# Stage 2's weight quarters over five chunks of stage 1, and the next chunk's tokens ahead of a chunk's last pairs

## The chip, the cores and the metric

The kernel runs on one core of a Trainium2 chip. The metric is the time of one execution on the device in microseconds, the median of several runs. The core has five engines, each with its own instruction queue that it works through in order: TensorE (PE in the profile), VectorE (DVE), ScalarE (ACT), GpSimd (POOL) and SyncE (SP), which here only issues DMAs. An engine waits on semaphores for results of the others; a waiting instruction holds up all that stands behind it in its queue.

## The reference

A windowed attention is followed by two gated feed-forward layers on its 2304 tokens. All inputs are float32.

```python
x = attention(q, k, v)                  # 4 batches, 8 heads, 576 positions, head size 64 -> [2304, 512]
a = x @ w1; b = x @ w2                  # 512 -> 1024
y = (a * b @ w3) @ w_out                # 1024 -> 1024 -> 512          (stage 1)
g = y @ w_gate; v2 = y @ w_val          # 512 -> 1536
out = (g * sigmoid(g) * v2) @ w_out2    # 1536 -> 512                  (stage 2)
```

## The kernel before

Every float32 matrix is split into a high and a low float32r part, and each product is made of three matmuls (high by high, high by low, low by high: `mm3`, L207 to L212). The high part is an ACT copy and the low part a subtraction, on DVE for tokens (`to_parts`, L156) and on POOL for weights.

The attention runs in units of a head pair: scores (PE), softmax (DVE, ACT, POOL), transposes (PE, with an ACT copy `pt` behind each), values (PE). Four head pairs are one batch of 576 tokens. The output of a head pair is written to the DRAM tensor `x1d` (L390); the first batch goes into `x` directly.

Stage 1 takes the tokens in five chunks, 0 to 4, of 512, 512, 512, 512 and 256 (`stage1`, eight steps `k` each). A step makes a gate on PE into one bank (`gate_a`, copied out by ACT as `ta`), a second into another (`gate_b`, multiplied by DVE, split into `p`), and 12 matmuls of the contraction of the step before. The contracted weights `W` were made of `w3` and `w_out` earlier. Results go to the DRAM tensor `x2d`. Between the gates of chunks 0 to 2 stand the attention units of batches 1 to 3, so that a batch is done at three quarters of a chunk. A chunk's tokens `x` are loaded from `x1d` into a raw buffer (`raw<-x1d`, L148) once that batch is written (`x1_there`), and split by `next_block` (ACT copies and DVE subtractions of 128x1024, two of each).

Stage 2 multiplies 2 x 2 blocks by seven products in place of eight (Strassen's scheme in Winograd's form). The seven sums of each weight block have to be made first: `quarters` takes one pair of weight blocks (`wg`, `wv` or `wo2`) from a raw buffer, rebuilds its float32 values from 64-bit input (ACT L193, DVE L194 and L195), adds quarters (DVE, L524 to L527), splits the results into a stage buffer (ACT L507, POOL L508) and stores them in DRAM (`wd` or `wod`, L545). There are 18 pairs, three for each of six blocks. In stage 2 a ring of 14 buffers is filled from `wd` (`fill`, L643), and `operands` makes the seven token operands from `x2d`, which needs both raw buffers.

Two things set the order around the change. The list `blocks` says in which order pairs and tokens are loaded; only two raw buffers exist after chunk 0 (three up to there), and a load is issued when a raw buffer comes free (`done_with`, `load_block`). And `rest(k)` and `replace(k)`, called behind each step of a chunk, take pieces of work from the queue `work`, three or two a step, the rest of a chunk's work in its last step. On DVE each piece stands behind the step's `p` (`tc.issue_after`). Within these bounds a scheduler at build time sets the order on each engine.

Of the kernel before, what the change touches and what calls it, by code (L numbers as in the profile page):

```python
# [11 lines left out]
F32R = mybir.dt.float32r  # L12
# [11 lines left out]
P = 128  # L24
# [8 lines left out]
K1 = F1 // P  # L33
# [19 lines left out]
N_W1 = len(W_ORDER)  # L53
for _k in range(0, K2, 2):
    W_ORDER += [(("wg", _k), ("wg", _k + 1)), (("wv", _k), ("wv", _k + 1)), (("wo2", _k), ("wo2", _k + 1))]
NW = len(W_ORDER)
# [25 lines left out]
NRING = 14  # L82

UNITS = [1, 1, 1, 1, 1, 1, 2]

def moe_chain_kernel(tc, q_in, k_in, v_in, w_in, mask_in, out):
# [8 lines left out]
    with static as st, other as ot, psum as pp, dram as dp:  # L97
# [18 lines left out]
        count = {"att": 0, "p": 0, "o": 0}  # L116


        blocks = [("w", i) for i in range(N_W1)] + [("x1", 1)]
        for c in (1, 2, 3):  # L120
            blocks += [("w", i) for i in range(N_W1 + 6 * (c - 1), N_W1 + 6 * c)] + [("x1", c + 1)]
        blocks += [("x2", (c, j)) for c in range(NC2) for j in range(2)]
        n_loaded, n_split = [0], [0]
        slot_of, pair_of, uses, raw_at = {}, {}, {}, {}
# [140 lines left out]
        with att1_pool as a1, att2_pool as a2:  # L265
# [6 lines left out]
            raw_pool = tc.tile_pool(name="rawx", bufs=1)  # L272
# [184 lines left out]
            for s in range(2 * K1):  # L457
                h, j = divmod(s, K1)
# [6 lines left out]
                for kk in range(4):  # L465
                    c = slice(kk * P, (kk + 1) * P)
# [13 lines left out]
            def stage1(c, between, after):  # L480
                first, n = CHUNKS[c]
                x = xb[c % 2][:, :, :, :n]
                for k in range(K1):
                    gate_a(("w1", k), x, n, AF.Copy)
                    between(3 * k + 1)
                    p = gate_b(("w2", k), x, n)
                    between(3 * k + 2)
                    flush()
                    between(3 * k + 3)

                    def fin(k=k, p=p):
                        contract(slot_of["W", k], p, n, k == 0, k == K1 - 1)
                        if k == K1 - 1:
                            drain(lambda m: x2d[m, :, first:first + n], n)

                    pend.append(fin)
                    after(k)

            def attend_in(c):
                lo, hi = done_at[c + 1], done_at[c + 2]  # L500
                return lambda n: attend(lo + math.ceil((hi - lo) * n / (3 * K1 * ATT_BY)) if n < 3 * K1 * ATT_BY else hi)
# [55 lines left out]
                    except StopIteration:  # L557
                        work.popleft()

            def rest(k):  # L560
                while n_split[0] < N_W1 and free:
                    next_block()
                for b in range(1, B):
                    if at[0] >= done_at[b + 1]:
                        x1_there.update({b} if b < B - 1 else {b, b + 1})
                load_block()
                if n_split[0] > N_W1:
                    if k == 0:
                        work.extend([quarters() for _ in range(6)])
                    step(99 if k == K1 - 1 else 3)  # L570
                if k == K1 - 1:
                    next_block()

            for c in range(3):
                stage1(c, attend_in(c), rest)
                if c == 0:
                    raw_pool.__exit__(None, None, None)
                    stage_pool = tc.tile_pool(name="stages", bufs=1)
                    sp = stage_pool.__enter__()
                    stages.extend(sp.tile([P, 1792], F32R, name=f"stage{i}") for i in range(2))  # L580
            stage_pool.__exit__(None, None, None)


# [2 lines left out]
        with mid_pool as mp:  # L586
# [57 lines left out]
                    n_ring[0] += 1  # L644

            def replace(k):
                if k == 2:
                    work.append(operands())
                if k >= 2:
                    step(99 if k == K1 - 1 else 2)  # L650

                fill({5: 10, 6: 12, 7: NRING}.get(k, 9))

            stage1(3, lambda n: None, rest)
            stage1(4, lambda n: None, replace)
            flush_first = pend.pop()
            fill()
# [184 lines left out]
```

## Time and profile before

| | us |
|---|---|
| median of 3 runs (lowest, highest) | 893.24 (892.51, 894.55) |
| the profiled execution | 895.88 |
| its span, first to last instruction | 894.1 |
| PE busy in it | 859.2 (96%) |
| DVE, ACT, POOL busy | 567.2, 351.4, 166.8 |
| chunk 0 of stage 1 on PE | about 98 to 187 |
| chunk 1, chunk 2 | 187 to 276, 276 to 362 |
| chunk 3, chunk 4 | 362 to 435, 435 to 481 |
| stage 2 | to the end |

The attention's scores start near 9 us, and up to 98 us `W` is made. An instruction's row names its line, its engine, its operation and what it writes and reads; in brackets stands how long the engine sat idle before it and what ended that. The granted clock is a share of TensorE's full 2.4 GHz.

### The profile page before, as it was taken

Reading aid. Unit: us, or ns where it says so; the run is one execution under the profiler, and the core shown is the slowest. Engines: PE = TensorE matmul, PEld = TensorE weight load, DVE = VectorE, ACT = ScalarE, POOL = GpSimd, SP = SyncE. Lnnn points to the kernel's source line nnn. Section 1 sums busy time; section 2 is a strip of 40 time slices with the busy share of each in tenths; the row PEclk is TensorE's granted clock in tenths of the full one; section 3 lists DMA queues with packets and bytes.
Section 4 is the critical chain, followed back from the end, with each engine's and each line's share of the span. In section 5 each row is a group of like instructions: output and inputs, shape, how many; then the busy total and the mean of one; then the engine's idle time right before and its main releaser. Section 6 shows DMA issues by size and latency. Waiting matters only on the chain.

```text
span 894.1 us, 13459 instructions
## 1 busy us (share of the span) xinstructions
PE 859.2 (96%) x5065; PEld 780.3 (87%) x5066; DVE 567.2 (63%) x968; ACT 351.4 (39%) x809; POOL 166.8 (19%) x149
## 2 busy tenths in 40 slices
PE   8889899999998989899899999999999999999998
PEld 5767688878887878688799999999999999999998
DVE  5887953355555643454365866678666687666766
ACT  5866753355646553434342322232222232222221
POOL 4556531015432533143200000000000000000000
PEclk9999799999999999899999999999999999999999
DMA  9886732259787767886948766687766667766311
GB/s 296 263 278 223 231 108 63 83 181 290 249 239 266 240 214 231 299 283 224 312 160 306 243 199 206 210 283 232 243 208 212 210 200 237 247 213 204 126 48 71
DMA packets 92433, 192.95 MB, mean 216 GB/s; under 512 B 6480, under 2 KB 56272, under 8 KB 87632
## 3 DMA queue, kind: packets, MB, share of 16 engines
q1 hardware_dynamic: 89488, 187.37, 64.4%
q10 hardware_dynamic: 2880, 4.72, 1.4%
q8 instruction: 40, 0.66, 0.3%
q14 instruction: 25, 0.20, 0.1%
HBM read 150.65 MB, written 41.42 MB: 215 GB/s over the span
## 4 chain that ended last, share of the span: by engine, by line
PE 64%; DMA 17%; ACT 5%; DVE 5%; POOL 4%; issue 3%; SPq 1%; ACTq 0%; POOLq 0%; DVEq 0%
PE bk L210 20%; PE bk L211 20%; PE bk L212 20%; DMA raw<-w_in 8%; DMA raw<-x1d 3%; POOL stage L508 3%; DVE raw L195 2%; PE bk L312 2%; DMA wd<-mid 2%; DMA wd<-stage 1%; ACT raw L193 1%; DMA x1d<-o 1%; ACT s L331 1%; DVE raw L194 1%; PE bk L364 1%
## 5 line engine op out<-in xcount | busy, mean ns | idle before, releaser
L695 DVE TENSOR_TENSOR s<-bk,s 128x384 f32<-128x384 f32 x252 | 137.5, 554 | 48.9 <-PE bk L212 28.5
L210 PE MATMUL bk<-x,w 128*128 128x512 f32 (+2 forms) x368 | 139.7, 382 | 11.5 <-ACT x L157 11.3
L211 PE MATMUL bk<-x,w 128*128 128x512 f32 (+2 forms) x368 | 139.4, 379 | 1.7 <-DVE x L158 1.6
L212 PE MATMUL bk<-x,w 128*128 128x512 f32 (+2 forms) x368 | 138.3, 376 | 0.0
L212 PE MATMUL bk<-p,wo 128*128 128x384 f32 x288 | 97.3, 338 | 0.0
L210 PE MATMUL bk<-p,wo 128*128 128x384 f32 x288 | 96.8, 337 | 0.0
L211 PE MATMUL bk<-p,wo 128*128 128x384 f32 x288 | 96.8, 336 | 0.0
L737 DVE TENSOR_TENSOR acc<-bk,acc 128x384 f32<-128x384 f32 x120 | 66.5, 554 | 43.9 <-PE bk L212 43.5
L210 PEld LDWEIGHTS bk<-x,w 128*128 128x128 f32 x368 | 71.6, 196 | 23.7 <-ACT x L157 12.8
L698 ACT ACTIVATE s<-s 128x384 f32<-128x384 f32 x72 | 37.8, 526 | 129.6 <-DVE s L695 128.5
L211 PEld LDWEIGHTS bk<-x,w 128*128 128x128 f32 x368 | 71.5, 194 | 13.1 <-DVE x L158 3.5
L212 PEld LDWEIGHTS bk<-x,w 128*128 128x128 f32 x368 | 71.7, 195 | 9.9
L157 ACT ACTIVATE p<-s 128x384 fp32r<-128x384 f32 x72 | 37.7, 526 | 102.6 <-DVE s L699 102.6
L235 DVE TENSOR_TENSOR ta<-bk,ta 128x512 f32<-128x512 f32 (+1 forms) x40 | 25.4, 636 | 75.2 <-PE bk L212 47.6
L210 PE MATMUL bk<-w 128*128 128x384 f32 (+1 forms) x196 | 70.3, 366 | 2.3 <-ACT w L188 2.0
L211 PE MATMUL bk<-w 128*128 128x384 f32 (+1 forms) x196 | 69.7, 360 | 0.5 <-POOL w L189 0.5
L211 PE MATMUL bk<-w,mid 128*128 128x384 f32 x204 | 68.6, 336 | 0.0
L212 PE MATMUL bk<-w,mid 128*128 128x384 f32 x204 | 67.9, 337 | 0.0
L210 PE MATMUL bk<-w,mid 128*128 128x384 f32 x204 | 67.8, 336 | 0.0
L212 PE MATMUL bk<-w 128*128 128x384 f32 (+1 forms) x196 | 67.4, 356 | 0.0
L508 POOL TENSOR_TENSOR stage<-raw,stage 128x512 fp32r<-128x512 f32 (+2 forms) x56 | 52.4, 962 | 75.2 <-ACT stage L507 75.2
L195 DVE SCALAR_TENSOR_TENSOR raw<-raw 128x1024 uint32<-128x1024 uint32 (+1 forms) x39 | 59.2, 1519 | 9.5 <-ACT raw L193 8.2
(99 smaller groups left out, 1756.3 us busy)
## 6 DMA issues: line engine op xcount, KB each, us to landing
raw<-w_in SPq DMA_DIRECT2D x37, 1024.0 KB, 7.6
mid<-wd SPq DMA_DIRECT2D x72, 512.0 KB, 4.3
w<-wd SPq DMA_DIRECT2D x45, 512.0 KB, 3.5
wo<-wod SPq DMA_DIRECT2D x36, 512.0 KB, 4.5
wd<-stage SPq DMA_DIRECT2D x16, 896.0 KB, 6.6
wd<-mid SPq DMA_DIRECT2D x8, 896.0 KB, 5.9
v<-v_in SPq DMA_DIRECT2D x16, 432.0 KB, 5.3
q<-q_in SPq DMA_DIRECT2D x32, 160.0 KB, 6.2
```

The costliest lines, as they stand in the source:

```text
L157: nc.scalar.activation(hi, src, AF.Copy)
L193: nc.scalar.activation(hi.bitcast(F32), hi.bitcast(F32), AF.Prelu, scale=REBIAS, alpha=SIGN_UP)
L195: nc.vector.scalar_tensor_tensor(out=lo, in0=hi, scalar=3, in1=lo, op0=ALU.logical_shift_left, op1=ALU.bitwise_or)
L210: nc.tensor.matmul(ps, wh, xh, start=start, stop=False)
L211: nc.tensor.matmul(ps, wh, xl, start=False, stop=False)
L212: nc.tensor.matmul(ps, wl, xh, start=False, stop=stop)
L235: nc.vector.tensor_tensor(out=u, in0=bb[:, :n], in1=ta[:, :n], op=ALU.mult)
L312: nc.tensor.matmul(ps[:, (n - b0) * KW:(n - b0 + 1) * KW], q[:, QB + 2 * QB * n:QB + 2 * QB * (n + 1)], kk[:, n * QB:n * QB + KW], start=T ...
L508: nc.gpsimd.tensor_tensor(out=dst[:, :, 1], in0=src, in1=dst[:, :, 0].bitcast(F32), op=ALU.subtract)
L695: nc.vector.tensor_tensor(out=dst[m], in0=x[m], in1=y[m], op=ALU.add)
L698: nc.scalar.activation(u[0], u[0], AF.Silu)
L737: nc.vector.tensor_tensor(out=a, in0=ps, in1=a, op=ALU.add)
```

## The change

The 18 pairs are dealt out by the list `QUARTERS`: 3, 4, 4, 5 and 2 to chunks 0 to 4, in place of 6 each to chunks 1 to 3. In `blocks` a chunk's pairs come ahead of the next chunk's tokens, but in chunk 3 the tokens of chunk 4 come first, so that they are loaded right behind chunk 3's own and split in step 1 of chunk 3. Quarters begin in step 2 of chunk 0 (by then the stage 1 weights are converted and the third raw buffer is given up for the two stage buffers), in step 0 of chunks 1, 2 and 4 and in step 1 of chunk 3. In chunk 4 `operands` stands behind the last two pairs, and the ring is filled with 4 buffers up to step 2 and 9 from step 3, since stage buffers in `mid` overlap it.

```diff
@@ -83,6 +83,7 @@
 
 UNITS = [1, 1, 1, 1, 1, 1, 2]
 
+QUARTERS = [3, 4, 4, 5, 2]
 
 
 def moe_chain_kernel(tc, q_in, k_in, v_in, w_in, mask_in, out):
@@ -116,9 +117,15 @@
         count = {"att": 0, "p": 0, "o": 0}
 
 
-        blocks = [("w", i) for i in range(N_W1)] + [("x1", 1)]
-        for c in (1, 2, 3):
-            blocks += [("w", i) for i in range(N_W1 + 6 * (c - 1), N_W1 + 6 * c)] + [("x1", c + 1)]
+        blocks = [("w", i) for i in range(N_W1)]
+        i = N_W1
+        for c, n in enumerate(QUARTERS):
+
+            x1 = [("x1", c + 1)] if c < 4 else []
+            w = [("w", i + j) for j in range(n)]
+            blocks += x1 + w if c == 3 else w + x1
+            i += n
+        assert i == NW
         blocks += [("x2", (c, j)) for c in range(NC2) for j in range(2)]
         n_loaded, n_split = [0], [0]
         slot_of, pair_of, uses, raw_at = {}, {}, {}, {}
@@ -557,27 +564,31 @@
                     except StopIteration:
                         work.popleft()
 
-            def rest(k):
+            def rest(c, k):
                 while n_split[0] < N_W1 and free:
                     next_block()
                 for b in range(1, B):
                     if at[0] >= done_at[b + 1]:
                         x1_there.update({b} if b < B - 1 else {b, b + 1})
                 load_block()
-                if n_split[0] > N_W1:
-                    if k == 0:
-                        work.extend([quarters() for _ in range(6)])
+                begin = (2, 0, 0, 1)[c]
+                if k == begin:
+                    if c == 0:
+                        assert n_split[0] == N_W1
+                        raw_pool.__exit__(None, None, None)
+                        sp = stage_pool.__enter__()
+                        stages.extend(sp.tile([P, 1792], F32R, name=f"stage{i}") for i in range(2))
+                    if c == 3:
+                        next_block()
+                    work.extend([quarters() for _ in range(QUARTERS[c])])
+                if k >= begin:
                     step(99 if k == K1 - 1 else 3)
-                if k == K1 - 1:
+                if k == K1 - 1 and c < 3:
                     next_block()
 
+            stage_pool = tc.tile_pool(name="stages", bufs=1)
             for c in range(3):
-                stage1(c, attend_in(c), rest)
-                if c == 0:
-                    raw_pool.__exit__(None, None, None)
-                    stage_pool = tc.tile_pool(name="stages", bufs=1)
-                    sp = stage_pool.__enter__()
-                    stages.extend(sp.tile([P, 1792], F32R, name=f"stage{i}") for i in range(2))
+                stage1(c, attend_in(c), lambda k: rest(c, k))
             stage_pool.__exit__(None, None, None)
 
 
@@ -644,14 +655,13 @@
                     n_ring[0] += 1
 
             def replace(k):
-                if k == 2:
-                    work.append(operands())
-                if k >= 2:
-                    step(99 if k == K1 - 1 else 2)
-
-                fill({5: 10, 6: 12, 7: NRING}.get(k, 9))
-
-            stage1(3, lambda n: None, rest)
+                if k == 0:
+                    work.extend([quarters() for _ in range(QUARTERS[4])] + [operands()])
+                step(99 if k == K1 - 1 else 4 if k < 2 else 2)
+
+                fill({5: 10, 6: 12, 7: NRING}.get(k, 9 if k > 2 else 4))
+
+            stage1(3, lambda n: None, lambda k: rest(3, k))
             stage1(4, lambda n: None, replace)
             flush_first = pend.pop()
             fill()
```

On each engine the built program changes as follows; lines of the changed kernel are seven to ten higher. PE at the passage from chunk 1 to chunk 2, before (L312 and L349 are attention scores and transposes; `p,W` is the contraction, `x_76` the tokens of chunk 2):

```order
L212 MATMUL bk_84<-p,W_75 128x512
L210 MATMUL bk_85<-p,W_75 128x512
L211 MATMUL bk_85<-p,W_75 128x512
L212 MATMUL bk_85<-p,W_75 128x512
L349 MATMUL bk_89<-ident,s_110 96x128 x3
L210 MATMUL bk_86<-x_76,w 128x512
L210 MATMUL bk_87<-x_76,w 128x512
L349 MATMUL bk_88<-ident,s_110 96x128 x3
L211 MATMUL bk_86<-x_76,w 128x512
L212 MATMUL bk_86<-x_76,w 128x512
```

And in the changed kernel:

```order
L219 MATMUL bk_85<-p,W_75 128x512
L319 MATMUL bk_89<-k_103,q_101 128x96 x4
L217 MATMUL bk_86<-x_76,w 128x512
L319 MATMUL bk_89<-k_103,q_101 128x96
L319 MATMUL bk_88<-k_103,q_101 128x96 x3
L218 MATMUL bk_86<-x_76,w 128x512
L219 MATMUL bk_86<-x_76,w 128x512
L217 MATMUL bk_86<-x_76,w 128x512
L218 MATMUL bk_86<-x_76,w 128x512
L219 MATMUL bk_86<-x_76,w 128x512
L217 MATMUL bk_86<-x_76,w 128x512
L319 MATMUL bk_88<-k_103,q_101 128x96
```

Before, both contractions, all scores and three transposes of 96x128 stand ahead of the first matmul on `x`; now the second contraction of 12 matmuls, five of the nine score matmuls' rows and the transposes stand behind it.

SP at the same place, before (`x1d<-o_80` is the last attention output that chunk 2 needs, `raw_79<-x1d` the load of its tokens):

```order
L545 DMA wd<-stage_1386 896x1x256
L297 DMA v<-v_in 96x9x128
L545 DMA wd<-stage_1387 896x1x256
L390 DMA x1d<-o_80 128x576
L545 DMA wod<-stage_1386 128x1024
L148 DMA raw_79<-x1d 128x4x512
L545 DMA wod<-stage_1387 128x1024
```

And in the changed kernel:

```order
L552 DMA wd<-stage_1046 896x1x256
L552 DMA wd<-stage_1047 896x1x256
L155 DMA raw_79<-w_in 128x2048
L296 DMA q_100<-q_in 64x5x128 x2
L299 DMA k_102<-k_in 128x576
L304 DMA v<-v_in 96x9x128
L397 DMA x1d<-o_80 128x576
L155 DMA raw_78<-x1d 128x4x512
```

The stores of quarters have moved ahead of the outputs of the last head pair, and the token load follows its output directly.

SP at the passage from chunk 2 to chunk 3, before (from the last attention output on; `mid<-wd` are the first fills of the ring):

```order
L390 DMA x1d<-o_80 128x576
L545 DMA wd<-stage_1386 896x1x256
L545 DMA wd<-stage_1387 896x1x256
L148 DMA raw_78<-x1d 128x4x512
L545 DMA wod<-stage_1386 128x1024
L545 DMA wod<-stage_1387 128x1024
L148 DMA raw_79<-w_in 128x2048
L643 DMA mid<-wd 128x1024 x2
L148 DMA raw_78<-w_in 128x2048
L643 DMA mid<-wd 128x1024 x2
```

And in the changed kernel:

```order
L397 DMA x1d<-o_81 128x576
L552 DMA wd<-stage_1046 896x1x256
L552 DMA wd<-stage_1047 896x1x256
L654 DMA mid<-wd 128x1024 x2
L397 DMA x1d<-o_80 128x576
L654 DMA mid<-wd 128x1024 x2
L155 DMA raw_79<-x1d 128x4x512
L155 DMA raw_78<-x1d 128x4x256
L155 DMA raw_79<-w_in 128x2048
L155 DMA raw_78<-w_in 128x2048
```

The load of chunk 3's tokens is no longer behind two stores, but two of the four fills are ahead of the last attention output and two behind it, and chunk 4's tokens (128x4x256) follow chunk 3's at once.

ACT in chunk 4, before, from step 0's `ta` on (`x_67`, `w` 128x768 are stage 2's operands, from `raw` or from sums `tx`):

```order
L229 ACTIVATE ta<-bk_86 128x256
L252 ACTIVATE o_81<-bk_82 128x512
L157 ACTIVATE p<-ta 128x256
L157 ACTIVATE x_67<-raw_78 128x768
L255 DMA x2d<-o_81 128x512
L255 DMA x2d<-o_80 128x512
L229 ACTIVATE ta<-bk_86 128x256
L157 ACTIVATE p<-ta 128x256
L157 ACTIVATE w<-raw_79 128x768
L229 ACTIVATE ta<-bk_86 128x256
L157 ACTIVATE w<-raw_79 128x768
L252 ACTIVATE o_81<-bk_84 128x512
```

And in the changed kernel, from the last copy of the last pair (`mid<-raw_79`) to the `ta` of step 6:

```order
L514 ACTIVATE mid<-raw_79 128x512
L236 ACTIVATE ta<-bk_86 128x256
L164 ACTIVATE x_67<-raw_78 128x768
L164 ACTIVATE w<-tx_2759 128x768
L164 ACTIVATE p<-ta 128x256
L236 ACTIVATE ta<-bk_86 128x256
L164 ACTIVATE p<-ta 128x256
L164 ACTIVATE w<-raw_79 128x768 x2
L714 ACTIVATE s_2761<-bk_88 128x384
L164 ACTIVATE x_67<-tx_2760 128x768
L164 ACTIVATE w<-tx_2759 128x768
L236 ACTIVATE ta<-bk_86 128x256
```

The first operand has moved from step 0 to step 4, behind the copies of the last pair, and those from the second raw buffer (`raw_79`), which stood on both sides of step 2's `ta`, stand ahead of step 6's.

## Rows read from the trace of the kernel before

**Rows 1.** The page: busy us, share of the span and instructions, PE.

```profile
PE 859.2 (96%) x5065; PEld 780.3 (87%) x5066; DVE 567.2 (63%) x968; ACT 351.4 (39%) x809; POOL 166.8 (19%) x149
```

**Rows 2.** Timeline of PE: start, duration, instruction, idle before it and releaser.

```profile
186.72 0.73 PE L210 MATMUL bk<-x,w 128*128 128x512 f32 x2 [1.56 <-ACT x L157]
187.98 0.80 PE L211 MATMUL bk<-x,w 128*128 128x512 f32 x1 [0.52 <-DVE x L158]
...
276.53 1.17 PE L210 MATMUL bk<-x,w 128*128 128x512 f32 x2 [2.29 <-ACT x L157]
...
362.65 1.22 PE L210 MATMUL bk<-x,w 128*128 128x512 f32 x2 [3.42 <-ACT x L157]
...
435.42 0.50 PE L210 MATMUL bk<-x,w 128*128 128x256 f32 x2 [3.56 <-ACT x L157]
```

**Rows 3.** Windows: us, busy and count of PE, PEld, DVE, ACT, POOL; PEclk, DMA, GB/s.

```profile
187.00:191.20 4.20, 3.68 (x10) 2.57 (x10) 2.92 (x5) 3.28 (x12) 0.83 (x1) 0.60 0.56 140
276.53:280.00 3.47, 3.47 (x10) 2.74 (x11) 3.47 (x5) 3.47 (x15) 0.00 (x0) 0.51 1.07 295
362.65:368.80 6.15, 6.11 (x14) 4.32 (x15) 2.94 (x3) 2.58 (x3) 0.00 (x0) 0.50 0.98 346
437.00:440.40 3.40, 3.40 (x15) 3.01 (x14) 0.30 (x1) 0.00 (x0) 0.00 (x0) 0.51 0.86 252
375.00:400.00 25.00, 25.00 (x112) 20.71 (x111) 15.68 (x21) 11.23 (x22) 12.37 (x13) 1.00 0.74 240
445.00:450.00 5.00, 5.00 (x44) 5.00 (x43) 0.85 (x2) 2.22 (x5) 0.00 (x0) 1.00 0.96 353
```

**Rows 4.** Timeline of PE in chunk 2: the longest of four waits for `pt`.

```profile
329.18 0.80 PE L364 MATMUL bk<-pt,v 96*64 96x32 f32 x20 [1.13 <-ACT pt L351]
```

**Rows 5.** The chain that ended last, in order of time: start, us, what.

```profile
176.93 3.27 DMA x1d<-o
180.22 5.38 DMA raw<-x1d
185.62 1.06 ACT x L157
...
261.67 7.44 DMA x1d<-o
269.12 6.28 DMA raw<-x1d
...
351.73 9.79 DMA raw<-x1d
```

**Rows 6.** Timeline: attention's last values into chunk 2, and SP's stores behind attention.

```profile
255.78 1.39 PE L364 MATMUL bk<-pt,v 96*64 96x64 f32 x40
...
260.36 1.20 SPq L545 DMA_DIRECT2D wd<-stage  x1
...
343.82 0.33 SPq L390 DMA_DIRECT2D x1d<-o  x1
```

**Rows 7.** DMA issues: queue, count, KB each, median us to landing.

```profile
mid<-wd SPq DMA_DIRECT2D x72, 512.0 KB, 4.3
...
wd<-mid SPq DMA_DIRECT2D x8, 896.0 KB, 5.9
...
raw<-x2d SPq DMA_DIRECT2D x6, 768.0 KB, 6.4
...
x1d<-o SPq DMA_DIRECT2D x12, 288.0 KB, 4.3
```

**Rows 8.** Timelines of ACT and POOL: an operand's copy in chunk 4; one pair's subtractions.

```profile
448.39 0.85 ACT L157 ACTIVATE w<-raw 128x768 fp32r<-128x768 f32 x1 [1.20 <-DMA raw<-x2d]
...
377.22 5.26 POOL L508 TENSOR_TENSOR mid<-raw,mid 128x256 fp32r<-128x256 f32 x6 [17.26 <-ACT mid L507]
```

**Rows 9.** Timeline of DVE: low half of `p`, POOL idle and POOL busy.

```profile
178.49 0.69 DVE L158 TENSOR_TENSOR p<-ta,p 128x512 fp32r<-128x512 f32 x1 [0.70 <-ACT p L157]
...
259.32 1.47 DVE L158 TENSOR_TENSOR p<-ta,p 128x512 fp32r<-128x512 f32 x1 [0.70 <-ACT p L157]
```

## The prediction

> **What bounds the kernel now.** I read the busy shares first, then TensorE's own timeline for every wait in it, then windows for the clock, then the chain of work behind each long wait. PE is busy 96% of 894.1 us [rows 1], so only stages in which PE stands idle or runs slowly can give anything back. From 495 us on it hardly waits; all long waits lie where stage 1 passes from one chunk of tokens to the next. There PE waits for `x`, the next chunk's tokens: 1.56 + 0.52 us into chunk 1, 2.29 into chunk 2, 3.42 into chunk 3 and 3.56 into chunk 4 [rows 2], 11.35 us in sum. Behind each of them the granted clock is at half, 1.2 GHz, for a while: 0.60 over 4.20 us, 0.51 over 3.47, 0.50 over 6.15, 0.51 over 3.40 [rows 3]. What such a stretch costs is its length times one minus the clock: 1.68, 1.70, 3.07, 1.67, together 8.1. So the four passages cost 3.8, 4.0, 6.5 and 5.2 us, **19.5 us** in all. PE also waits four times inside chunk 2's attention, 2.5 us together, 1.13 the longest [rows 4].
>
> What delays `x` differs. Into chunk 1 nothing stands before it: the last attention output is stored at 176.93, its landing releases the load at 180.22, ACT copies at 185.62 [rows 5]: the bare chain, with DMA otherwise quiet. Into chunk 2 the attention ends on PE at 257.17, but SP still issues a `wd` store at 260.36 [rows 6]; the `x1d` store goes out at 261.67 and takes 7.44 us to land, against 3.27 into chunk 1 [rows 5]. Into chunk 3 the store is out at 343.82 [rows 6], yet the load starts at 351.73, since it needs a raw buffer that the quarter pairs still hold, and takes 9.79 us [rows 5]. Into chunk 4 the load stands behind all six pairs of chunk 3, though its data were stored before that chunk began.
>
> **The change, part by part.** The work is the same: 18 pairs, the same matmuls, the same 4 token loads. Before, chunks 1 to 3 hold 6 pairs each; now chunks 0 to 4 hold 3, 4, 4, 5 and 2.
>
> *Into chunk 4.* The tokens are fetched right behind chunk 3's, a whole chunk ahead, and split in chunk 3. The wait and its slow stretch go: **5.2**. The split (two ACT copies, two DVE subtractions) moves into chunk 3, where ACT and DVE wait for PE; if that cover went, it would cost again what it costs now.
>
> *Into chunk 2.* On SP nothing of the quarters stands any more between the last attention output and the token load. From the end of the attention the store is out after about 1.5 us (ACT's half of the output), lands in 3.3 (as into chunk 1) to 4.3 (the median [rows 7]), the load takes 5.4 to 6.3 and ACT's copy 1.06 [rows 5]: 11.3 to 13.2 us. PE's cover: before, 17.07 us lay between 257.17 and PE's running dry at 274.24 (276.53 less 2.29). The new order puts 12 matmuls, 5 of 9 score steps and three transposes behind the first `x` matmul; at 0.223 us a matmul (112 in 25.00 us [rows 3]) that takes 2.7, and some 1.1 and 0.5 for the others, away: 12.8. So PE waits 0 to 0.4, or up to the full 4.0 if the store again takes 7.4. I keep 1.0 of the 4.0: **3.0**.
>
> *Into chunk 1.* The cover grows: before, 8.23 us from the store's issue to 185.16 (186.72 less 1.56); the order now has ten more matmuls in it and three transposes fewer, 10.0. The chain from the issue is 3.3 + 5.4 + 1.06 = 9.8, if the three new pairs keep away from it. They do on SP: their stores are all ahead of the last attention output. I keep 0.5 of 3.8: **3.3**; at worst all stays.
>
> *Into chunk 3.* The load no longer waits for the last pairs, but four ring fills of 512 KB now stand around the last `x1d` store, two before, two behind it. Cover from the store's issue: 15.4 us (343.82 to 359.23, which is 362.65 less 3.42) less 13 matmuls that moved behind, 12.5. The chain: 3.3 to 4.3, 5.4 to 6.3 and 1.06, so 9.8 to 11.7; it fits, unless the fills add to it. I keep 1.5 of 6.5 for that: **5.0**; at worst all stays. What is late next there is the attention itself. A row and a rule bear on it: the load that shared its time with stores and weights took 9.79 us against 5.38 in the quiet [rows 5]. The Trainium skill, DMA: Bandwidth & Descriptors, section Queues, rings and completion order, says that on each DMA engine the descriptors of a ring are consumed in ring order; by that the two fills behind the store are ahead of the load whatever SP does. The trace agrees in kind, 9.79 against 5.38; if one fill's 4.3 us [rows 7] were added to the chain, 2 to 3.5 us of wait would stay there and the forecast would be some 2 us higher.
>
> *Inside the attention.* Chunks 1 and 2 have two pairs fewer; I take half of the 2.5 us of waits as gone, **1.2** (between none and all). Chunk 0 has three pairs more, beside attention that had no such wait. Chunk 1 took six pairs without one, chunk 2 took six with 2.5. For half as many: cost **0.6**, between 0 and 2.5.
>
> *Chunk 4* is the only place where something new can be late. It lasts some 46 us, its matmuls take 0.114 us each (44 in 5.00 [rows 3]), and two pairs now come ahead of the first operands of stage 2, in the same two raw buffers. All from its start, estimated from rows: PE wants operand 0 after 12 matmuls of the chunk before and 180 of its own, 2.7 + 20.5 = 23.2. The pair `wv` goes through DVE behind the first `p`, at about 5; POOL's six subtractions, 5.3 us [rows 8], are done at 14; the first half of `x2d` is then fetched, 6.4 [rows 7], and lands at 21; ACT's copy, 0.85 [rows 8], is done at 22.5: just in time. The pair `wo2` waits for `wv`'s stores to land, 14 + 5.9 [rows 7]; its two copies and POOL are done near 23.5, the other half of `x2d` lands at 30, and on ACT five copies then stand ahead of `ta` of k = 6, which comes at 34.5. PE wants it at 2.7 + 240 x 0.114 + 16 stage-2 matmuls of 384 columns (0.17 each, in proportion) = 32.8. Cost **1.5**, from 0.5 to 8 (a load of 10 us and a slow stretch behind the wait); below zero is out, as PE has no wait there to lose.
>
> Sum: 5.2 + 3.0 + 3.3 + 5.0 + 1.2 - 0.6 - 1.5 = **15.6 us**. The profiled run took 895.88 (its span 894.1), 2.6 above the median of 893.24; taken from the median this gives 877.6, say **877.5 us**.
>
> **The rivals.** *A, the chain and not the queue was late*: into chunks 1 and 3 the load still hangs on the last attention output, and nothing comes earlier there. For it: into chunk 1 no pair was in the way. Against it: the longer cover. 5.0 and 3.3 stay: 885.9. This is also the case in which the change does only half of what it says.
>
> *B, stage 2's operands come late in chunk 4*: ACT stands in front of `x2d`, and PE behind ACT. For it: the margins above are under 2 us, and before, ACT already stood 1.20 us for `x2d` [rows 8] with all of chunk 4 to hide it. 6 to 10 us instead of 1.5: 882 to 886.
>
> *C, slower*: quarters beside attention cost more than the passages did. Place: chunks 0 to 2, ACT, DVE and POOL in the softmax of 12 head pairs. Its price is the wait of chunk 2, 2.5 us for one head pair; from seven head pairs on (17.5) the gain is gone, with all twelve the time is 877.5 + 30 = 907. For it: DVE's low half of `p` took 1.47 us with POOL's subtractions beside it and 0.69 without [rows 9]. Against it: six pairs a chunk showed this wait once. The Trainium skill, SBUF — State Buffer, section Who interferes with whom, states that a DVE instruction with two SBUF inputs contends with a GpSimd instruction that reads SBUF. The trace agrees, 0.78 us an instruction; by the rule alone, with all eight `p` of chunk 0 exposed, 6.2 us are lost instead of 0.6 and the time is 883.
>
> **How the numbers follow.** Forecast (871 to 882) 0.56; A 0.17; B 0.14; C 0.08, of which 0.02 ends within the bound; a mixture of A and B that eats all, 0.05, half within it, half slower. The best case takes all of 19.5 + 2.5: 871.2. A and B end near 886; with some room for both in part, the range is 871 to 887, and leaves out C, the mixture and a little of B. What a measurement of this kernel can tell from no change is about 0.2%, 1.8 us. Faster 0.87, same 0.045, slower 0.085.
>
> **What would show it.** In the profile after: no PE wait for `x` into chunk 4, token loads of 5 to 7 us into chunks 1 to 3 with PE waits under 1.5 us each, and a granted clock of 1.00 behind them. B would show as PE waits for `ta` or for operands in chunk 4, with ACT waiting for `raw<-x2d`; C as waits for ACT `pt` in chunks 0 to 2; A as waits for ACT `x` of 1.5 us or more into chunks 1 and 3. A wait into chunk 4 would make the first step wrong.

## The result, and the profile after

The changed kernel takes **882.43 us** (median of 6 runs, 880.95 to 885.8) against 893.24 us before (892.51 to 896.17): a ratio of 0.9878, 95% interval 0.9856 to 0.9900, so 10.8 us less. Its profiled execution took 881.68 us with a span of 879.9; that of the kernel before took 895.88 and 894.1. So the two profiles lie 14.2 us apart, more than the medians; what of this is explained stands near the end.

The page of the changed kernel, busy time of each engine:

```profile
PE 851.8 (97%) x5065; PEld 774.9 (88%) x5066; DVE 567.8 (65%) x968; ACT 349.3 (40%) x809; POOL 166.4 (19%) x149
```

PE is busy 7.4 us less than in [rows 1] for the same number of instructions, as it runs at half clock less often (the ledger below has the time). The timeline of PE at the four passages, the places of [rows 2]:

```profile
189.74 0.71 PE L217 MATMUL bk<-x,w 128*128 128x512 f32 x2
...
271.25 0.48 PE L217 MATMUL bk<-x,w 128*128 128x512 f32 x1
...
357.69 0.62 PE L217 MATMUL bk<-x,w 128*128 128x512 f32 x2
...
420.41 0.28 PE L217 MATMUL bk<-x,w 128*128 128x256 f32 x1
```

No row has a bracket: PE no longer waits for `x` at any passage (no wait there is over 0.15 us). The windows behind them, to be set beside the first four of [rows 3] (columns as there; the last but two is the granted clock):

```profile
189.70:193.70 4.00, 4.00 (x21) 3.17 (x20) 3.41 (x6) 4.00 (x19) 0.39 (x1) 1.00 0.55 198
271.25:275.25 4.00, 4.00 (x25) 3.49 (x25) 3.33 (x7) 1.50 (x9) 0.00 (x0) 1.00 0.60 203
357.70:363.70 6.00, 6.00 (x27) 4.78 (x26) 4.18 (x7) 2.83 (x6) 0.00 (x0) 1.00 0.72 223
420.40:424.40 4.00, 4.00 (x30) 3.81 (x29) 1.17 (x2) 1.40 (x4) 0.89 (x1) 1.00 0.77 211
```

The clock is 1.00 (2.4 GHz) where it was 0.50 to 0.60. The chain into chunks 1 and 2, for [rows 5]:

```profile
179.81 3.28 DMA x1d<-o
...
183.10 5.20 DMA raw<-x1d
...
188.33 1.07 ACT x L164
...
260.67 2.43 DMA x1d<-o
...
263.16 5.16 DMA raw<-x1d
```

Into chunk 1 the chain is as long as it was (3.28 + 5.20, before 3.27 + 5.38); PE has more work to cover it, 9.93 us from the store's issue at 179.81 to the first `x` matmul at 189.74, of which store, load and copy take 9.55. Into chunk 2 it shrank from 7.44 + 6.28 to 2.43 + 5.16.

New waits stand inside the chunks. The timeline of PE in chunk 0 (the waits of more than half a microsecond) and in chunk 4:

```profile
152.75 0.53 PE L356 MATMUL bk<-ident,s 128*96 128x128 f32 x3 [0.63 <-DVE s L333]
...
158.00 0.53 PE L356 MATMUL bk<-ident,s 128*96 128x128 f32 x3 [1.28 <-ACT pt L358]
...
163.59 1.36 PE L319 MATMUL bk<-k,q 128*128 128x96 f32 x10 [0.90 <-ACT o L394]
...
431.43 0.38 PE L217 MATMUL bk<-x,w 128*128 128x256 f32 x1 [1.65 <-ACT ta L236]
...
436.65 0.74 PE L217 MATMUL bk<-p,W 128*128 128x256 f32 x4 [0.78 <-ACT p L164]
```

With one more of 0.23, chunk 0 has 3.0 us of them, chunk 4 has 2.4. Chunks 1 and 2 have 0.36, 1.13 and 0.39. What ACT does there, its timeline:

```profile
145.17 1.21 ACT L514 ACTIVATE stage<-raw 128x512 fp32r<-128x512 f32 x3 [5.44 <-DMA wd<-stage]
...
153.17 1.18 ACT L200 ACTIVATE raw<-raw 128x1024 f32<-128x1024 f32 x1 [2.39 <-DMA raw<-w_in]
...
162.32 0.66 ACT L514 ACTIVATE stage<-raw 128x512 fp32r<-128x512 f32 x1 [1.50 <-DMA wd<-stage]
162.88 0.66 ACT L394 ACTIVATE o<-bk 128x288 f32<-128x288 f32 x1
...
430.48 0.63 ACT L514 ACTIVATE mid<-raw 128x256 fp32r<-128x256 f32 x2 [2.51 <-DMA wd<-mid]
431.01 0.36 ACT L236 ACTIVATE ta<-bk 128x256 f32<-128x256 f32 x1
433.56 1.15 ACT L200 ACTIVATE raw<-raw 128x1024 f32<-128x1024 f32 x1 [2.18 <-DMA raw<-w_in]
```

ACT works through its queue in order. A copy into a staging buffer (L514) waits until the buffer's last store has landed, a rebuild of raw weights (L200) until its load has; `o`, `pt`, `ta` and `p`, for which PE waits, stand behind (the 1.65 us at 431.43 end with `ta` at 431.01, which had stood behind the 2.51 us wait for a store). The Trainium skill, TensorE: Matmul & The Clock Gate, section Architectural detail, calls the queues of ScalarE and VectorE strictly first in, first out; these rows agree.

**A ledger of both losses.** From the windows view in steps of 2 us from 96 to 500 us I added, for each kernel, the time in which PE was not busy (idle) and the length times one minus the granted clock (slow). The span less both is 862 to 868 us for all of them, so nearly everything that tells these kernels apart is in the two columns. From 96 to 110 us, where chunk 0 starts and no copy of a pair is made yet (the first is at 135 us in the changed kernel), they lose 6.0 to 8.2 us, of which 3.4 or 5.1 at half clock; the change has nothing to do with it.

| kernel | pairs in chunks 0 to 4 | ratio to before (95%) | span | idle | slow |
|---|---|---|---|---|---|
| before | 0 6 6 6 0 | 1 | 894.1 | 16.3 | 13.5 |
| changed | 3 4 4 5 2 | 0.9878 (0.9856–0.9900) | 879.9 | 10.2 | 3.4 |
| e1 tokens first alone | 0 6 6 6 0 | 1.0006 (0.9992–1.0021) | 894.8 | 19.6 | 8.5 |
| e2 spread alone | 3 4 4 5 2 | 0.9871 (0.9846–0.9896) | 886.4 | 13.6 | 6.8 |
| e3 | 0 5 5 6 2 | 0.9958 (0.9939–0.9976) | 887.9 | 15.2 | 5.1 |
| e4 | 3 4 4 7 0 | 1.0074 (1.0051–1.0096) | 901.5 | 22.5 | 17.1 |
| q | 2 4 5 5 2 | 0.9947 (0.9923–0.9972) | 893.1 | 15.5 | 11.9 |
| q | 3 4 5 5 1 | 1.0009 (0.9985–1.0033) | 894.8 | 18.3 | 10.2 |
| copies on GpSimd, chunks 3, 4 | 3 4 4 5 2 | 0.9926 (0.9902–0.9949) | 887.8 | 14.6 | 6.8 |
| copies on GpSimd, all | 3 4 4 5 2 | 0.9891 (0.9855–0.9926) | 884.3 | 9.2 | 11.9 |
| changed, again | 3 4 4 5 2 | 0.9868 (0.9843–0.9893) | 880.4 | 10.4 | 3.4 |
| e2, again | 3 4 4 5 2 | 0.9859 (0.9835–0.9882) | 879.9 | 9.5 | 5.1 |
| no first fill | 3 4 4 5 2 | 0.9901 (0.9880–0.9922) | 885.0 | 11.4 | 8.5 |
| copies on GpSimd, chunks 1, 2 | 3 4 4 5 2 | 0.9846 (0.9821–0.9870) | 879.3 | 7.4 | 6.8 |

The last four were measured together, against the same runs of the kernel before, so their ratios can be set beside each other. A kernel's profiled execution need not be its median one: e2's two profiles differ by 6.5 us, its two ratios by 0.0012.

### The profile page after: what moved, and what is told of

Same layout as the page of the kernel before. It is cut to its first block, busy times and chain, and to the rows that moved or that the text cites. A ratio compares the mean times of both kernels' runs of the same rounds, so it can differ in the third digit from the quotient of the medians.

```text
span 879.9 us, 13463 instructions
## 1 busy us (share of the span) xinstructions
PE 851.8 (97%) x5065; PEld 774.9 (88%) x5066; DVE 567.8 (65%) x968; ACT 349.3 (40%) x809; POOL 166.4 (19%) x149
## 4 chain that ended last, share of the span: by engine, by line
PE 61%; DMA 15%; DVE 8%; ACT 6%; issue 4%; POOL 4%; SPq 2%; ACTq 0%; DVEq 0%; POOLq 0%
PE bk L219 19%; PE bk L218 19%; PE bk L217 19%; DMA raw<-w_in 9%; DVE raw L202 3%; ACT s L338 2%; POOL stage L515 2%; DVE raw L201 2%; ACT raw L200 2%; PE bk L319 2%; DMA q<-q_in 2%; DMA wd<-stage 1%; DMA raw<-x1d 1%; POOL mid L515 1%; POOL w L196 1%
## 5 line engine op out<-in xcount | busy, mean ns | idle before, releaser
L217 PE MATMUL bk<-x,w 128*128 128x512 f32 (+2 forms) x368 | 136.1, 371 | 2.5 <-ACT ta L236 1.6
L218 PE MATMUL bk<-x,w 128*128 128x512 f32 (+2 forms) x368 | 136.3, 370 | 1.6 <-DVE x L165 1.6
L219 PE MATMUL bk<-x,w 128*128 128x512 f32 (+2 forms) x368 | 136.3, 370 | 0.0
L217 PEld LDWEIGHTS bk<-x,w 128*128 128x128 f32 x368 | 69.7, 190 | 12.5 <-ACT ta L236 1.9
L218 PEld LDWEIGHTS bk<-x,w 128*128 128x128 f32 x368 | 69.8, 190 | 12.0 <-DVE x L165 2.6
L219 PEld LDWEIGHTS bk<-x,w 128*128 128x128 f32 x368 | 69.8, 190 | 9.5
L165 DVE TENSOR_TENSOR p<-ta,p 128x512 fp32r<-128x512 f32 (+1 forms) x40 | 33.5, 838 | 46.0 <-ACT p L164 45.9
```

The lines of the kernel that those rows point to most:

```text
L165: return nc.vector.tensor_tensor(out=lo, in0=src, in1=hi.bitcast(F32), op=ALU.subtract)
L217: nc.tensor.matmul(ps, wh, xh, start=start, stop=False)
L218: nc.tensor.matmul(ps, wh, xl, start=False, stop=False)
L219: nc.tensor.matmul(ps, wl, xh, start=False, stop=stop)
```

## Experiments: the two halves of the change

**Tokens first alone.** The kernel before, with chunk 4's tokens split ahead of chunk 3's pairs, which then begin in step 1, as in the changed kernel (the main lines of the edit):

```diff
-            blocks += [("w", i) for i in range(N_W1 + 6 * (c - 1), N_W1 + 6 * c)] + [("x1", c + 1)]
+            w = [("w", i) for i in range(N_W1 + 6 * (c - 1), N_W1 + 6 * c)]
+            blocks += [("x1", c + 1)] + w if c == 3 else w + [("x1", c + 1)]
...
+                    if c == 3 and k == 1:
+                        next_block()
```

> The kernel before with one change: in chunk 3 the tokens of chunk 4 are loaded and split ahead of the six weight pairs (6, 6, 6 pairs in chunks 1 to 3 as before). Theory (the queue alone made the wait into chunk 4): PE's wait of 3.56 us into chunk 4 and the half-clock stretch behind it (1.67) go, the three other passages keep theirs (2.1, 2.3 and 3.4 us): about 888.0 against 893.2, ratio 0.994. Rival (the six pairs behind the tokens now end later and make chunk 4 or the stage behind it wait for operands): a new wait of 3 to 5 us in chunk 4, 892 to 893, ratio 0.999 to 1.000.

Measured: ratio 1.0006, no change. The wait for `x` into chunk 4 is gone, but the six pairs behind the tokens now reach to the end of the chunk and beyond. Timelines of PE and of ACT, at the start of chunk 4:

```profile
434.84 0.39 PE L211 MATMUL bk<-x,w 128*128 128x256 f32 x1 [1.88 <-ACT ta L230]
```

```profile
430.30 0.63 ACT L508 ACTIVATE mid<-raw 128x256 fp32r<-128x256 f32 x2 [4.46 <-DMA wd<-mid]
433.67 0.63 ACT L508 ACTIVATE mid<-raw 128x256 fp32r<-128x256 f32 x2 [2.73 <-DMA wd<-mid]
434.21 0.58 ACT L230 ACTIVATE ta<-bk 128x512 f32<-128x512 f32 x1
```

ACT waits 4.46 and 2.73 us for stores, `ta` stands behind, PE waits 1.88 for it; four more waits of 0.43 to 1.27 follow up to 491 us. These five come to 5.1 us. The wait changed its name: the rival holds.

**Spread alone.** The changed kernel with the tokens back behind chunk 3's pairs:

```diff
-            blocks += x1 + w if c == 3 else w + x1
+            blocks += w + x1
...
-                    if c == 3:
-                        next_block()
...
-                if k == K1 - 1 and c < 3:
+                if k == K1 - 1:
                     next_block()
```

> The changed kernel with chunk 4's tokens again behind chunk 3's pairs (3, 4, 4, 5, 2 pairs as in the change). Theory (tokens first is what frees the passage into chunk 4): a PE wait of 3 to 3.6 us and a half-clock stretch come back there, and nothing else changes: 882.4 + 5 = 887 to 888, ratio 0.994. Rival (one pair fewer in chunk 3 already shortens the queue enough): wait under 1 us, 882 to 883, ratio 0.988.

> The changed kernel with chunk 4's tokens behind chunk 3's pairs, on the same chip as the changed kernel itself. Theory of the prediction (tokens first is worth 5.2 us): 0.6% slower than the changed kernel. Rival (five pairs in place of six already free the passage into chunk 4, and tokens first is worth at most the wait of 1.3 us that this kernel showed at the passage into chunk 3): within 0.3% of it.

Measured: 0.9871, and beside the changed kernel on one chip 0.9859 against 0.9868. Tokens first is worth nothing that can be measured; 0.6%, the price in my prediction, is outside both intervals. Timelines of SP and PE of this kernel, and below them SP's row of the kernel before:

```profile
408.07 0.42 SPq L155 DMA_DIRECT2D raw<-x1d  x1
```

```profile
426.18 0.28 PE L217 MATMUL bk<-x,w 128*128 128x256 f32 x1
```

```profile
427.23 1.37 SPq L148 DMA_DIRECT2D raw<-x1d  x1
```

With five pairs the load goes out 18.1 us ahead of the first matmul on `x`; with six it went out 8.2 us ahead of one that had by then waited 3.56 us for it (435.42 in [rows 2]). So the spread alone frees the passage. That it is the one pair less in chunk 3 is the nearest reading; no run takes out that pair and nothing else. The 1.3 us into chunk 3 in its first profile are not in its second.

## Experiments: how many pairs, and where

**None in chunk 0.**

```diff
-QUARTERS = [3, 4, 4, 5, 2]
+QUARTERS = [0, 5, 5, 6, 2]
```

> The changed kernel with 0, 5, 5, 6 and 2 pairs. Chunk 0 has no pair, and the order of TensorE's matmuls around the passages into chunks 1, 2 and 3 is again that of the kernel before. Theory O (the matmuls that the schedule moved behind the first use of the new tokens are what covers the chain of store and load there): the waits come back nearly whole, 2.1, 2 and 3 us, with half clock behind them, some 3.8 + 4 + 6 us, while chunk 0 gets back its 3.3 us of waits: 891 to 893, ratio 0.997 to 1.000. Theory Q (fewer pairs in front of a passage make the chain shorter, order or not): only the passage into chunk 1 waits (2.1 us, 3.8 with the clock), those into 2 and 3 under 1 us each: 882.4 - 3.3 + 3.8 + 2 = 884 to 886, ratio 0.990 to 0.992.

Measured 0.9958, between the two theories. PE's timeline at the passages into chunks 1 and 2; below it the chain into chunk 2, and what SP issues ahead of it:

```profile
188.79 0.73 PE L217 MATMUL bk<-x,w 128*128 128x512 f32 x2 [2.23 <-ACT x L164]
...
277.15 0.73 PE L217 MATMUL bk<-x,w 128*128 128x512 f32 x2 [0.85 <-ACT x L164]
```

```profile
262.24 6.95 DMA x1d<-o
...
269.20 6.81 DMA raw<-x1d
```

```profile
260.08 0.56 SPq L552 DMA_DIRECT2D wd<-stage  x1
```

From 110 us on chunk 0 is free of waits again. Into chunk 1 the order of matmuls is that of before, and so is the wait, with half clock behind it. Into chunks 2 and 3 PE has no more work ahead of its first use of `x` than before either, apart from three transposes, and yet 0.85 + 0.53 us and nothing are left. Into 3 that is the number of pairs: the load goes out at 345.22, 2.1 us behind its store, where before it waited for a raw buffer until 351.73. Into 2 five pairs free the passage only in part: a `wd` store still goes out just ahead of the attention output, and store and load take 6.95 + 6.81 us, as long as before (7.44 + 6.28). With four pairs, in the changed kernel, SP issues no store of quarters within 8 us ahead of that output, and they take 2.43 + 5.16. So Q holds into 3, O into 1, and into 2 neither as it stands. What I had not reckoned with: six pairs in chunk 3 behind the tokens bring 3.5 us of waits in chunk 4 and 1.6 at the start of stage 2, and five in chunk 2 bring 2.2 in its attention.

**None in chunk 4.**

```diff
-QUARTERS = [3, 4, 4, 5, 2]
+QUARTERS = [3, 4, 4, 7, 0]
```

> The changed kernel with 3, 4, 4, 7 and 0 pairs: chunk 4 splits no weights, chunk 3 seven pairs behind the tokens. Theory (the waits of 1.65 and 0.78 us in chunk 4 are ScalarE held up by the last pairs' staging and load): both go, nothing comes in their place in chunk 3, whose passage into 4 is free of the queue: 880, ratio 0.985. Rival (seven pairs do not fit in chunk 3; what is left is pushed to its end, and TensorE waits there for ScalarE or for p): 2 to 4 us of new waits at the end of chunk 3 or early in chunk 4, 882 to 885, ratio 0.988 to 0.991.

Measured 1.0074, far worse than either. Timelines of PE and ACT, and the chain that ended last:

```profile
440.17 0.58 PE L217 MATMUL bk<-p,W 128*128 128x256 f32 x1 [8.17 <-ACT o L259]
```

```profile
433.96 0.66 ACT L514 ACTIVATE mid<-raw 128x512 fp32r<-128x512 f32 x1 [2.79 <-DMA wd<-mid]
...
436.35 1.17 ACT L200 ACTIVATE raw<-raw 128x1024 f32<-128x1024 f32 x1 [1.21 <-DMA raw<-w_in]
439.52 0.60 ACT L259 ACTIVATE o<-bk 128x512 f32<-128x512 f32 x1 [2.00 <-DMA x2d<-o]
```

```profile
425.10 8.78 DMA wd<-mid
```

Seven pairs do not fit into chunk 3, so the last one is worked off in chunk 4 all the same. A store ahead of its copies takes 8.78 us to land, and behind ACT's three waits PE stands 8.17 us, with 6.8 more lost at half clock up to 450 us. Five more waits of 0.49 to 2.24 us, most of them for stage 2's operands, follow up to 464 us. Taking the pairs out of chunk 4 made chunk 4 worse.

**One pair moved**, out of chunk 0 or out of chunk 4 into chunk 2:

```diff
-QUARTERS = [3, 4, 4, 5, 2]
+QUARTERS = [2, 4, 5, 5, 2]
...
-QUARTERS = [3, 4, 4, 5, 2]
+QUARTERS = [3, 4, 5, 5, 1]
```

> The changed kernel with 2, 4, 5, 5 and 2 pairs: one pair moved from chunk 0 to chunk 2. Theory (a pair in chunk 0 costs about 1.1 us of waits, and five pairs in chunk 2 are still few enough for the passage into chunk 3): 881 to 882, ratio 0.986 to 0.987. Rival (the fifth pair in chunk 2 brings back waits in its attention and at the passage behind it): 2 to 4 us back, 884 to 886, ratio 0.990 to 0.992.

> The changed kernel with 3, 4, 5, 5 and 1 pairs: one pair moved from chunk 4 to chunk 2. Theory (chunk 4's waits come from the last pair's load and staging stores beside the first operands of the next stage): the waits of 2.4 us in chunk 4 go, some 1 us comes back in chunk 2: 881, ratio 0.986. Rival (chunk 2 with five pairs loses what chunk 4 gains, or more): 882 to 885, ratio 0.988 to 0.991.

Measured 0.9947 and 1.0009: both slower than theory and rival. Timelines of PE, in chunks 0 and 2, and of ACT, in chunk 0, of the first, and PE's of the second, in chunk 4:

```profile
165.92 2.45 PE L319 MATMUL bk<-k,q 128*128 128x96 f32 x10 [3.08 <-ACT o L394]
...
289.58 0.50 PE L217 MATMUL bk<-x,w 128*128 128x512 f32 x1 [2.74 <-ACT ta L236]
```

```profile
164.21 1.10 ACT L200 ACTIVATE raw<-raw 128x1024 f32<-128x1024 f32 x1 [4.80 <-DMA raw<-w_in]
165.22 0.66 ACT L394 ACTIVATE o<-bk 128x288 f32<-128x288 f32 x1
```

```profile
451.26 0.58 PE L217 MATMUL bk<-x,w 128*128 128x256 f32 x1 [3.83 <-DVE w L165]
```

Two pairs in chunk 0 cost more than three: the rebuild of a pair's weights now stands directly ahead of the last `o` of a head pair and waits 4.80 us for its load; PE waits 3.08, and 3.4 us go at half clock. The rival came true as well: with five pairs chunk 2 has 4.7 us of waits (2.74, and 0.52 and 1.46 for `pt`), and 2.8 stand in chunk 4. In the second, the passage into chunk 3 waits 1.9 us again, chunk 4's waits do not go (1.44 for `ta` is the first), and the operands of stage 2 come late: 3.83 us, with 5.1 more at half clock behind. A pair has no price of its own; what it costs hangs on which copy stands behind its waits.

## Experiments: is it ScalarE's queue?

The first half of each weight split was given to GpSimd, which waits for the staging buffer in ScalarE's place. It was done in chunks 3 and 4, in all chunks, and in chunks 1 and 2; the edit is shown for all chunks, the two others make the same choice by the chunk:

```diff
-                nc.scalar.activation(dst[:, :, 0], src, AF.Copy)
+                nc.gpsimd.tensor_copy(dst[:, :, 0], src)
                 nc.gpsimd.tensor_tensor(out=dst[:, :, 1], in0=src, in1=dst[:, :, 0].bitcast(F32), op=ALU.subtract)
```

> The changed kernel, but in chunks 3 and 4 the first half of every weight split (a copy into the staging buffer) is made by GpSimd, not by ScalarE. Theory H (ScalarE works in its written order; a copy that waits for a staging buffer, whose store is still on its way, holds the `ta` and `o` copies of the chunk's gates behind it): the waits of 1.65 and 0.78 us in chunk 4 shrink to what the wait for the weight load alone holds (under 1 us in all): 880 to 881 where the changed kernel gives 882.4 (ratio 0.986). Rival (TensorE waits there because VectorE or the transfers are late): the waits stay, or grow, since GpSimd takes longer than ScalarE for a copy: 882 to 885, ratio 0.988 to 0.990.

> The changed kernel with GpSimd making the first half of every weight split in all chunks. Theory H: the four waits of chunk 0 (0.23, 0.63, 1.28 and 0.90 us) behind ScalarE's waits for a staging buffer go too, if GpSimd's own work in the attention (scaling the scores) does not wait behind its copies; 878 to 880, ratio 0.983 to 0.985. Rival (GpSimd's copies now stand ahead of its scaling of the scores, and slow VectorE beside them): waits of TensorE for `pt` and for `s` in chunks 0 to 2 of 1 to 3 us each, 10 us or more in all: 890 or slower, ratio 0.996 or more.

> The changed kernel with GpSimd making the first half of the weight splits in chunks 1 and 2 alone, where ScalarE's hold costs 0.36, 1.13 and 0.39 us of waits and where the run with GpSimd in all chunks showed none; chunks 0, 3 and 4 as in the changed kernel. Theory: 1.5 to 2 us faster than the changed kernel, ratio 0.984 to 0.987. Rival (the slower copies make a passage's tokens late, as that run's wait of 2.0 us into chunk 1 may say): 2 to 4 us of waits at a passage, ratio 0.990 to 0.992.

With all copies on GpSimd (0.9891) no wait of more than 0.3 us is left in the attention of chunks 0 to 2: the 3.0 us of chunk 0 and the 1.9 us of chunks 1 and 2 are gone, though GpSimd does more beside VectorE. Theory H holds there and its rival fell. Its time did not come, though: 878 to 880 us were forecast, a ratio of 0.983 to 0.985, and the kernel is no faster than the changed one. What is left, in PE's timeline:

```profile
188.61 0.74 PE L217 MATMUL bk<-x,w 128*128 128x512 f32 x2 [1.52 <-ACT x L164]
...
432.65 0.58 PE L217 MATMUL bk<-p,W 128*128 128x256 f32 x1 [3.01 <-DVE o L261]
```

The schedule put the first matmuls of chunk 1 where they stood before, and the wait for `x` is back with the pairs still in chunk 0, while store and load take 3.26 + 5.34 us as before: into chunk 1 it is the order that frees the passage. In chunk 4 theory H fell in both kernels; with GpSimd in chunks 3 and 4 alone the ratio is 0.9926, slower than theory and rival. In both, 1.7 to 1.8 us of waits for stage 2's operands come on top. PE now waits 3.0 us (2.96 with GpSimd in chunks 3 and 4 alone) for another copy, and VectorE's timeline of the kernel with all copies on GpSimd shows why:

```profile
431.91 0.69 DVE L261 COPY o<-bk 128x512 f32<-128x512 f32 x1 [5.28 <-DMA x2d<-o]
```

The copy waits until its buffer's last store to `x2d` has landed. With ScalarE freed, the next instruction that hangs on a transfer is what holds PE.

In chunks 1 and 2 alone: ratio 0.9846, as the theory has it, with no wait over 0.2 us left in them, while those of chunk 0 stay. It has the lowest ratio of all; beside the changed kernel measured with it (0.9868) its gain of 0.2% lies within the intervals.

**Less traffic in chunk 4.** The first load of the ring left out:

```diff
-                    nc.sync.dma_start(out=dst...
+                    if n_ring[0]:
+                        nc.sync.dma_start(out=dst...
```

> The changed kernel without the first of stage 2's weight loads, the 512 KB that are issued at the end of chunk 3 (stage 2 then computes with what stands in that buffer; nothing else is left out). Theory (chunk 4's waits come from a full DMA: the last pairs' stores and load land late because 3.4 MB are under way in 10 us, and ScalarE, held by them, holds TensorE): 0.5 MB less is 1.3 to 1.5 us earlier landing, and of the waits of 1.65 and 0.78 us under 1 us is left: 881, ratio 0.986. Rival (the waits come from the order on ScalarE alone, whatever the traffic): they stay, 882.4, ratio 0.988.

Measured 0.9901, slower than the changed kernel. ACT's timeline, and a piece of the chain that ended last:

```profile
433.46 1.14 ACT L200 ACTIVATE raw<-raw 128x1024 f32<-128x1024 f32 x1 [6.93 <-DMA raw<-w_in]
...
434.47 0.61 ACT L259 ACTIVATE o<-bk 128x512 f32<-128x512 f32 x1
```

```profile
426.56 7.27 DMA x2d<-o
```

The load of weights took 9.3 us in place of 11.0, but the schedule turned the order round as well: on ACT the rebuild and `o` now stand ahead of the `ta` that came first, and PE waits 3.74 us for `o`, with half clock behind. The rebuild is not all that holds `o`: a store to `x2d` that the chain shows ahead of it landed only at 433.8, 0.6 us before `o` began. So the experiment does not separate traffic from order. It shows that a load that lands 1.7 us faster helps nobody if another order and a slow store stand beside it.

**The changed kernel again:**

> The changed kernel once more, on the same chip as the next three, so that it can be set beside them: ratio 0.986 to 0.990 to the kernel before. If short waits (1.1 to 1.7 us) that stand just short of halving the clock explain why single runs of it spread over 5 us, its profile now shows some of them with half clock behind them; if not, the waits have gone and the spread is elsewhere.

Ratio 0.9868. In chunks 0 and 4 its waits stand at the same places, some a little longer (2.08 us at 431.49, 1.56 at 159.33), and no slow stretch is behind them.

## Why the prediction was right, and where it was not

The forecast of 877.5 lies 4.9 us below the measured 882.4, which is inside the range; the sign is right, and so is the place that the time came from, the passages. By the step:

- **The four passages** were to give 16.5 of 19.5 us and gave all of it. I had kept 0.5, 1.0 and 1.5 us for chunks 1 to 3, none of which was needed; into chunk 1 by a margin of 0.4 us.
- **Into chunk 4** the step was right in size (5.2) and wrong in its reason. I put it down to the tokens standing first. That does free the passage, but alone it gives 0, since the same time is lost behind it (e1); and without it the passage is just as free (e2, twice). The spread of the pairs is what gives the time. That the size came out right is luck.
- **Into chunks 2 and 3** the pairs were the cause, as said. Into 3, five pairs are few enough with before's order (e3). Into 2, the chain shrank by 6.1 us while the new order took cover away, so the order cannot have freed it; e3 shows that five pairs are not few enough, 1.4 us of wait and the long chain stay.
- **Into chunk 1** the longer cover was the cause, as said. Three kernels with before's order wait there 2.0 to 2.8 us, whether chunk 0 holds pairs or not (e1, e3, copies on GpSimd); those with the new order wait 0.2 us at most.
- **The fills into chunk 3.** The DMA issues of the changed kernel from 340 to 365 us (KB each, median us to landing):

```profile
raw<-x1d SPq DMA_DIRECT2D x1, 1024.0 KB, 5.2
...
x1d<-o SPq DMA_DIRECT2D x1, 288.0 KB, 5.3
```

  The store took 5.3 us, against 3.28 and 2.43 into chunks 1 and 2, so it was slower beside the fills; the load took 5.2, as into chunk 1, and PE waited nothing. The forecast that I drew from the rule of ring order, 2 us more, did not come: the two fills behind the store did not delay the load, which went out 4.9 us after them (350.56 against 345.65). From the store's issue at 345.23 the chain took 11.6 us of the 12.5 of cover that I had reckoned with. The 9.79 against 5.38 that I gave for the rule shows a load beside other traffic, not an order in a ring.
- **Inside attention, chunks 1 and 2**: 1.2 forecast; 2.7 us of waits (2.5 in chunk 2, one of which was for `o` and not for `pt`, and 0.16 in chunk 1) became 1.9, so about 0.8.
- **Chunk 0**, the step that was most mis-sized: 0.6 forecast (0 to 2.5), 3.0 measured, outside the bounds. I counted pairs and took half of what chunk 2 had shown. I did not ask what stands behind the staging copies on ACT.
- **Chunk 4**: 1.5 forecast, 2.4 measured. I let the wait fall late, at step 6, behind the copies for stage 2's operands, and took 5.9 and 6.4 us for transfers from the medians. It came within the first 16 us, behind a store and a load that took 11.0 us. The operands were in time: ACT waited 0.96 and 2.21 us for `raw<-x2d`, PE not at all.

With the measured terms the sum is 19.5 + 0.8 - 3.0 - 2.0 (2.4 less 0.4 that was there before) = 15.3. That this is close to the 15.6 forecast is luck: kept residues and mis-sized costs cancel. By the ledger the gain is 16.2 (29.8 less 13.6); the spans lie 14.2 apart, the rest being before 96 us, where PE reached chunk 0 1.1 us later, and the span outside the ledger.

The medians show 10.8, in the last group of runs 11.8 (895.65 against 883.82). The 4.9 us by which the forecast missed are for the smaller part the sum (15.6 against 14.2 between the profiles) and for the larger part its base: I took losses that I had read in an execution 2.6 us over the median off the median, and the changed kernel's profile lies 0.75 under its own. How much one execution can hold shows in e1, which waits into chunk 3 much as before (3.01 + 0.38 us), with half as much lost at half clock behind it, 1.7 us against 3.07. Its window there:

```profile
364.80:368.80 4.00, 3.58 (x9) 2.48 (x10) 3.98 (x5) 2.61 (x4) 0.00 (x0) 0.57 0.70 228
```

So 19.5 was a price of that execution, not of the kernel. The same shows in chunk 4: a wait of 2.22 us at 431.77 (e2 again) has half clock behind it, one of 2.08 at 431.49 (the changed kernel again) has not. Windows of the two:

```profile
432.00:436.00 4.00, 4.00 (x24) 4.00 (x24) 3.90 (x8) 2.20 (x7) 2.66 (x4) 0.62 0.36 136
```

```profile
431.40:435.40 4.00, 3.73 (x28) 3.48 (x29) 1.12 (x2) 1.83 (x4) 0.80 (x2) 1.00 0.25 96
```

Such a stretch costs 1.5 (4.00 times 0.38) to 1.7 us. It does not explain why runs of the changed kernel lie up to 4.9 us apart: its run of 885.8 us and its run of 880.95 have the same mean clock, 0.986. That spread stays open.

Of the rivals, A fell: all four waits went. B came in part, in its place but not by its way. C's place was right for chunk 0; its price was 2.5 us a head pair, and chunk 0 lost 3.0 us in all four; its mechanism was wrong: with more work on GpSimd the waits went.

## What to carry to other kernels

Before background work is moved beside a critical stage, look at what stands behind each of its waiting instructions on the same engine: a copy that waits for a free staging buffer costs what the copies behind it are worth; by the ratios one pair moved cost 6 and 12 us here, two pairs 18, with the same instructions. A queue that delays a load is often freed by taking one item out of it; put the load first only if the items behind it have somewhere to go. And weigh a gain by all waits and slow-clock stretches from profile to profile, since a wait that goes at one place may come back at the next under another name.

## What the runs showed of the hardware

- A load of 1024 KB took 5.2 us to land into chunks 1 and 2 (tokens) and 11.0 in chunk 4 (weights; from 418 to 436 us 4.15 MB were moved in all); a store of 896 KB took 8.78 in the kernel with seven pairs in chunk 3. The page's median for the loads of weights, 7.6 in the kernel before, hides this.
- The clock fell to half behind waits of 1.44 us (e2, at 294 us: 0.72 over 6 us) and 1.52 us (all copies on GpSimd, into chunk 1, with 0.52 more behind it), and stayed at 1.00 behind others of 1.65 (the changed kernel), 1.56 and 2.08 (the same again) and 1.88 (e1).
- GpSimd's copy of 128x512 from float32 to fp32r took 0.71 us, ScalarE's 0.66. The Trainium skill, GPSIMD Engine Reference, Engine selection, says that its one-input operations run about at line rate; the trace agrees in that its copy is within a tenth of ScalarE's.
